# Where and on which queue a spectral mixing kernel loads its filters, and how it shares the products of its first batch

## Chip, cores, metric

One Trainium2 chip, one core of it. The metric is device microseconds of one execution. Three executions of the kernel before gave a median of 1016.6 us (1016.42 to 1018.65). "us" counts from the start of the core's span unless a duration is meant.

## The reference

Eight sequences of 3008 tokens and 256 channels are multiplied by one complex filter in the frequency domain (filters of 1505 frequencies by 256 channels, real and imaginary part in two float32 arrays), then go through an RMS norm and a SwiGLU feed-forward layer.

```python
X = np.fft.rfft(x, axis=1)                       # x: (8, 3008, 256)
y = np.fft.irfft(X * (filt_r + 1j*filt_i), n=3008, axis=1)
rms = np.sqrt(np.mean(y*y, axis=-1, keepdims=True) + 1e-06)
xn = y / rms * rms_g
g = xn @ w_gate                                  # (256, 1536)
out = (g / (1 + np.exp(-g)) * (xn @ w_val)) @ w_out
```

## The kernel before

The transform of 3008 = 47 x 64 points is done in two stages by matmuls. The data change their layout between stages by a "bounce" through a scratch tensor in HBM: they are stored from SBUF (`z_store`) and loaded again in another order (`t2_load`). The parts that matter here:

- `a_unit`: first stage, one matmul and a ScalarE copy. `z_store`, `t2_load`: the first bounce.
- `b_unit(b, i)`: second stage for two of 32 columns, then two products with the filters, `s1 = ps*fr` and `s2 = ps*fi`. `bi_unit`: the first inverse stage of these columns (matmuls `psi`, a ScalarE copy). `g_store`, `t4_load`: the second bounce.
- norm, then for each tile of 512 tokens twelve slots of gate, value and down matmuls. `pg` is a gate matmul. From the first `pg` on, the mixing of the batches 1 to 7 is interleaved with the feed-forward slots of the batch before. Batch 0 has nothing to hide behind; its time up to the first `pg` is the *prologue*.

The filters come in four chunks of eight columns (f0 to f3), each of a real and an imaginary tile of 128 partitions. Rows 0 to 23 and 32 to 54 are loaded, the second group in reversed order; `f_dup` copies the lower half of the partitions to the upper half.

```python
def b_unit(b, i):
    ps = bank(0 if b else i % 2, "psb").rearrange("p (a d) -> p a d", a=2)
    for u in range(2):                       # two matmuls into ps
        ...
    s1 = sp.tile([P, 2, D], FP16, tag="s1", name="s1")
    s2 = sp.tile([P, 2, D], FP16, tag="s2", name="s2")
    c, r = divmod(2 * i, KC)
    nc.vector.tensor_tensor(out=s1, in0=ps, in1=fr[c][:, r:r + 2, :], op=ALU.mult)
    if b == 0 and i % 2:                     # odd units of batch 0: ScalarE copies, GpSimd multiplies
        v = ...
        nc.scalar.activation(out=v, in_=ps, func=AXT.Copy)
        nc.gpsimd.tensor_tensor(out=s2, in0=v, in1=fi[c][:, r:r + 2, :], op=ALU.mult)
    else:
        nc.vector.tensor_tensor(out=s2, in0=ps, in1=fi[c][:, r:r + 2, :], op=ALU.mult)
    st[b]["s"][i] = (s1, s2)

def f_load(c):
    for src, dst in ((filt_r, fr), (filt_i, fi)):
        t = dst[c]
        nc.gpsimd.dma_start(t[0:24, :, :].rearrange("p a d -> p (a d)"),            # 24 rows, 192 KB
                            raw(src, c * KC, [[64 * D, 24], [1, KC * D]]))
        lo = 1 if c == 0 else 0
        for a, e in ((0, 16), (16, 23)):                                            # 16 rows, 7 rows
            nc.gpsimd.dma_start(t[32 + a:32 + e, lo:KC, :],
                                raw(src, 64 * (a + 1) - c * KC - lo,
                                    [[64 * D, e - a], [-D, KC - lo], [1, D]]))
        ...                                                                         # one column more for c == 0

def f_dup(c):
    nc.vector.tensor_copy(out=fr[c][HALF:P], in_=fr[c][0:HALF])
    nc.scalar.activation(out=fi[c][HALF:P], in_=fi[c][0:HALF], func=AXT.Copy)

# the prologue, cut: x on GpSimd's queue, f0 behind it, then
for c in range(NC):
    ...                                      # memsets of fr[c], fi[c]
    for i in range(3):
        a_unit(0, 3 * c + i)
    z_store(0, c)
gate(st[0]["t1"][3][0:1, 5, 0:1])            # GpSimd waits for the last first-stage tile
f_load(1)
...
for c in range(3):
    t2_load(0, c)
gate(st[0]["t2"][0][0:1, 0, 0:1])            # GpSimd waits for the first second load
f_load(2)
...
for i in range(17):
    if i < 16:
        b_unit(0, i)
    if i == 1:
        f_load(3)
    if i == 7:
        w_load(0)                            # half of the weights; the other half at i == 11
    if i == 15:
        for c in range(NXC):
            x_load(1, c)
    if i % 4 == 1 and i // 4 + 1 < NC:
        f_dup(i // 4 + 1)
    if i >= 1:
        bi_unit(0, i - 1)
        if i % 2 == 0:
            g_store(0, i // 2 - 1)
    if i == 4:
        t2_load(0, 3)
```

## Time and profile before

| event (read from the trace) | us |
|---|---|
| f0, f1, f2, f3 landed | 21.1, 27.4, 44.5, 50.3 |
| last z store landed | 28.1 |
| first second load issued, landed | 28.3, 32.2 |
| first product | 35.5 |
| last g store issued, landed | 71.5, 81.1 |
| first gate matmul (end of the prologue) | 94.4 |
| span | 1015.2 |

The windows view gives each engine's busy time in a stretch (with the number of instructions), the granted clock, the mean busy share of the 16 DMA engines, and what they moved. Of the kernel before:

```profile
core 0: us, PE busy (x) PEld busy (x) DVE busy (x) ACT busy (x) POOL busy (x), PEclk, DMA share, GB/s
4.00:20.00 16.00, 7.37 (x27) 2.83 (x27) 13.66 (x12) 8.15 (x16) 9.79 (x20) 1.00 1.04 233
20.00:28.00 8.00, 0.00 (x0) 0.00 (x0) 4.47 (x6) 1.91 (x1) 0.13 (x1) 1.00 0.88 193
28.00:36.00 8.00, 2.90 (x20) 2.12 (x20) 6.04 (x9) 2.06 (x4) 3.44 (x7) 1.00 1.03 193
36.00:44.00 8.00, 4.39 (x19) 2.81 (x20) 5.84 (x9) 4.77 (x6) 5.55 (x9) 1.00 0.91 108
44.00:52.00 8.00, 5.44 (x24) 3.48 (x24) 4.25 (x6) 5.13 (x7) 2.51 (x3) 1.00 0.87 170
...
62.00:74.00 12.00, 5.57 (x25) 3.01 (x22) 2.67 (x4) 3.93 (x7) 8.36 (x14) 1.00 1.17 190
74.00:96.00 22.00, 5.52 (x44) 3.64 (x45) 3.26 (x8) 3.85 (x7) 2.51 (x3) 1.00 0.55 133
96.00:200.00 104.00, 98.60 (x666) 61.40 (x665) 62.94 (x103) 63.97 (x113) 22.73 (x19) 0.98 0.47 109
```

After 96 us TensorE is busy 98.6 of 104 us: little is to be gained there. Before, it has little to do in any row.

The waits view (engine and line, what it waited for: us in total, times, longest), same kernel, 28 to 95 us:

```profile
PE psn L310 <- DMA t_588<-g_tmp: 13.9, 1, 13.9
...
PE psi L232 <- DMA wi<-wi_t: 3.8, 1, 3.8
...
PE psi L232 <- POOL s_364 L222: 2.2, 1, 2.2
...
PE psi L232 <- POOL s_556 L222: 1.9, 1, 1.9
...
PE psi L232 <- POOL s_461 L222: 1.7, 1, 1.7
PE psi L232 <- POOL s_396 L222: 1.7, 1, 1.7
```

TensorE's largest is the inverse bounce (13.9: the last g store alone took 9.66 us to land). The `psi <- POOL` waits of about 2 us come once in each pair of units: an odd unit goes VectorE product, ScalarE copy, GpSimd product, inverse, and only then the next unit's matmul. The GpSimd product itself, by the view of its source line (the three numbers are the shortest, median and longest duration in ns):

```profile
L222 POOL TENSOR_TENSOR s_326<-v,fi_118 x1: 1598/1598/1598, 38.1 to 38.1; 128x512 f16<-128x512 f32 x1
L222 POOL TENSOR_TENSOR s_364<-v,fi_118 x1: 1274/1274/1274, 43.4 to 43.4; 128x512 f16<-128x512 f32 x1
L222 POOL TENSOR_TENSOR s_396<-v,fi_119 x1: 1678/1678/1678, 47.4 to 47.4; 128x512 f16<-128x512 f32 x1
```

### The profile page before, as it was taken

How to read it: one execution, taken by the hardware profiler on the slowest of the kernel's cores; microseconds unless marked ns; L12 is line 12 of the kernel's file. 1: busy time of each engine (PE TensorE's matmuls, PEld its weight loads, DVE VectorE, ACT ScalarE, POOL GpSimd, SP SyncE). 2: the span in 40 equal slices, each digit the busy share in tenths (PEclk: the TensorE clock that was granted, in tenths of full speed). 3: DMA queues.
4: the chain of work that ended last, by engine and by line, in shares of the span. 5: the costliest groups of instructions: out<-in, count | busy, mean ns of one | idle time of the engine just before them, and what ended most of it. 6: DMA issues, size and time to landing. Idle time of an engine off the chain costs nothing.

```text
span 1015.2 us, 17359 instructions
## 1 busy us (share of the span) xinstructions
PE 932.0 (92%) x6279; PEld 570.4 (56%) x6279; DVE 601.0 (59%) x980; ACT 602.4 (59%) x1060; POOL 249.1 (25%) x221
## 2 busy tenths in 40 slices
PE   2444989999999999999999999999999999999997
PEld 1322556655665566655665566655665556656554
DVE  8632467645774477645775467645775467645554
ACT  4443755666655765567555765567656766566543
POOL 5460341032401232032411323031411322023200
PEclk9999999999999999999999999999999999999999
DMA  9994373325723474324824375314724343312211
GB/s 193 165 167 108 87 172 76 102 76 135 151 66 102 96 169 103 99 72 121 164 51 121 86 150 123 107 50 117 162 78 123 86 125 87 101 49 61 43 42 39
DMA packets 94565, 107.25 MB, mean 106 GB/s; under 512 B 17224, under 2 KB 69064, under 8 KB 94288
## 3 DMA queue, kind: packets, MB, share of 16 engines
q1 hardware_dynamic: 85104, 87.59, 33.1%
q0 software_dynamic: 8992, 17.77, 11.7%
q8 instruction: 49, 0.80, 0.3%
q10 hardware_dynamic: 384, 0.79, 0.3%
q14 instruction: 36, 0.29, 0.1%
HBM read 70.88 MB, written 49.90 MB: 119 GB/s over the span
## 4 chain that ended last, share of the span: by engine, by line
PE 75%; DMA 8%; ACT 5%; issue 4%; DVE 3%; POOL 2%; SPq 1%; ACTq 0%; DVEq 0%; POOLq 0%
PE pg L359 21%; PE pv L359 20%; PE psi L232 5%; PE psb L212 3%; PE psn L264 2%; ACT sq L273 1%; SPq L201 1%; PE psa L191 1%; DMA g_tmp<-t_579 1%; DMA xc<-in_x_dram 1%; DVE hh L364 1%; PE psq L281 1%; DMA fi_120<-in_filt_i_dram 1%; ACT y L271 1%; PE po_12769 L376 0%
## 5 line engine op out<-in xcount | busy, mean ns | idle before, releaser
L364 DVE TENSOR_TENSOR hh<-pv,sg 128x512 f16<-128x512 f32 (+1 forms) x576 | 390.9, 679 | 349.5 <-ACT sg L363 224.1
L363 ACT ACTIVATE sg<-pg 128x512 f16<-128x512 f32 (+1 forms) x576 | 340.6, 591 | 308.6 <-PE pg L359 306.2
L359 PE MATMUL pg<-xn,wg 128*128 128x512 f16 (+1 forms) x1152 | 340.1, 377 | 0.0
L359 PE MATMUL pv<-xn,wv 128*128 128x512 f16 (+1 forms) x1152 | 338.9, 376 | 0.0
L376 PEld LDWEIGHTS <-hh 128*128 128x128 f16 (+1 forms) x2304 | 221.6, 98 | 110.6 <-issue 33.2
L339 POOL TENSOR_TENSOR xn<-y,rb 128x1024 f16<-128x1024 f32 (+1 forms) x47 | 129.6, 2758 | 300.8 <-DMA rb<-r_tmp 231.2
L359 PEld LDWEIGHTS <-wv 128*128 128x128 f16 x1152 | 113.1, 98 | 132.0 <-issue 2.2
L293 POOL TENSOR_TENSOR rho<-u,mhalf 128x4 f32<-128x4 f32 x48 | 48.6, 1013 | 376.0 <-DVE u L291 361.0
L359 PEld LDWEIGHTS <-wg 128*128 128x128 f16 x1152 | 105.7, 98 | 21.6
L232 PEld LDWEIGHTS <-wi 128*128 128x128 f16 x512 | 52.1, 103 | 54.2 <-issue 14.7
L271 ACT ACTIVATE y<-psn,gsb 128x512 f32<-128x512 f32 (+1 forms) x94 | 64.3, 684 | 10.4 <-PE psn L264 5.3
L273 ACT ACTIVATE sq<-psn 128x512 f16<-128x512 f32 (+1 forms) x94 | 55.5, 591 | 0.0
L191 PE MATMUL psa<-xc,wa 128*128 128x512 f16 x96 | 37.5, 408 | 10.8 <-DMA xc<-in_x_dram 9.6
L212 PEld LDWEIGHTS <-wb 96*128 96x128 f16 x256 | 24.9, 105 | 36.0 <-issue 15.0
L175 POOL DMA_DIRECT2D xc<-in_x_dram x64 | 34.9, 561 | 0.8 <-POOLq L579 0.8
L281 PEld LDWEIGHTS <-sq 128*128 128x128 f16 (+1 forms) x384 | 17.5, 97 | 14.9 <-ACT sq L312 2.2
L281 PE MATMUL psq<-ones,sq 128*128 128x1 f16 (+1 forms) x384 | 17.7, 165 | 3.7 <-ACT sq L312 1.9
L191 PEld LDWEIGHTS <-wa 128*128 128x128 f16 x96 | 9.3, 100 | 19.3 <-issue 11.7
L425 PE MATMUL pst<-ident,wb 96*128 96x128 f16 x31 | 3.7, 313 | 11.6 <-DMA wb<-wb_t 11.6
L429 DVE TENSOR_SCALAR wi<-pst 64x512 f16<-64x512 f32 (+1 forms) x16 | 10.7, 672 | 5.5 <-ACT wi L427 5.2
L310 PE MATMUL psn<-wai,t_588 128*128 128x128 f16 x8 | 1.0, 308 | 13.9 <-DMA t_588<-g_tmp 13.9
L313 DVE TENSOR_SCALAR y<-psn,gsb 128x512 f32<-128x512 f32 x2 | 1.4, 746 | 19.7 <-ACT sq L312 19.7
(965 smaller groups left out, 1171.3 us busy)
## 6 DMA issues: line engine op xcount, KB each, us to landing
rb<-r_tmp SPq DMA_DIRECT2D x47, 256.0 KB, 4.0
xc<-in_x_dram POOLq DMA_DIRECT2D x56, 192.0 KB, 5.9
xc<-in_x_dram POOLq DMA_DIRECT2D x8, 160.0 KB, 6.6
wb<-wb_t SPq DMA_DIRECT2D x4, 192.0 KB, 5.6
wg<-in_moe_w_gate_dram POOLq DMA_DIRECT2D x2, 384.0 KB, 5.3
wv<-in_moe_w_val_dram POOLq DMA_DIRECT2D x2, 384.0 KB, 7.2
wo<-in_moe_w_out_dram POOLq DMA_DIRECT2D x2, 384.0 KB, 9.4
r_tmp<-rho SPq DMA_DIRECT2D x47, 2.0 KB, 2.1
```

Of the source, the lines that this page charges most:

```text
L191: nc.tensor.matmul(ps, wa, st[b]["x"][c][:, 2 * r:2 * r + 2, :], start=True, stop=True)
L212: nc.tensor.matmul(ps[:, u, :], wb[:, k, :], st[b]["t2"][k // KC][:, k % KC, :], start=True, stop=True)
L232: nc.tensor.matmul(ps[:, u, :], wi[:, 2 * i + u, q, :], s12[q][:, u, :], start=(q == 0), stop=(q == 1))
L271: nc.scalar.activation(out=y[:, dh, 0:w], in_=ps[:, 0:w], func=AXT.Identity, scale=gsb[:, dh:dh + 1])
L273: nc.scalar.activation(out=st[b]["sq"][m][:, dh, 0:w], in_=ps[:, 0:w], func=AXT.Square)
L281: nc.tensor.matmul(ps[0:w, q:q + 1], sq[:, dh, q * P:q * P + w], ones, start=(dh == 0), stop=(dh == 1))
L293: nc.gpsimd.tensor_tensor(out=rho, in0=u, in1=mhalf, op=ALU.pow)
L339: nc.gpsimd.tensor_tensor(out=xv[:, :, 0:nq], in0=yv[:, :, 0:nq], in1=rv[:, 0:nq].unsqueeze(1).to_broadcast([P, 2, nq, P]), op=ALU.mult)
L359: nc.tensor.matmul(ps[:, 0:w], wt[:, dt_, ts(jt, P)], xn[:, dt_, 0:w], start=(dt_ == 0), stop=(dt_ == 1))
L363: nc.scalar.activation(out=sg[:, 0:w], in_=pg[:, 0:w], func=AXT.Silu)
L364: nc.vector.tensor_tensor(out=hh[:, 0:w], in0=pv[:, 0:w], in1=sg[:, 0:w], op=ALU.mult)
L376: nc.tensor.matmul(po[s4 // 2][0:w, s4 % 2, :], hh[:, s4 * P:s4 * P + w], wo[:, jt, :], start=(jt == 0 and s4 % 2 == 0), stop=(jt == JT - ...
```

## The change

The intent is to empty the store window of filter traffic, to have the tables copied early, to let whole products alternate between VectorE and GpSimd, and to take the inverse off their round trip. So the filters leave GpSimd's queue and stand on SyncE's between the stores and the loads of the first bounce; GpSimd takes both products of odd units; the inverse runs three units behind; x of batch 1 and two thirds of the weights wait for the second bounce.

```diff
 b_unit:
-        nc.vector.tensor_tensor(out=s1, in0=ps, in1=fr[c][:, r:r + 2, :], op=ALU.mult)
+        eng = nc.vector
         if b == 0 and i % 2:
+            eng = nc.gpsimd
             ...                      # ScalarE copies ps to v
+            ps = v
+        eng.tensor_tensor(out=s1, in0=ps, in1=f1, op=ALU.mult)
+        eng.tensor_tensor(out=s2, in0=ps, in1=f2, op=ALU.mult)
 f_load: each of its transfers
-            nc.gpsimd.dma_start(
+            nc.sync.dma_start(
 prologue:
+            if c == 1:               # tables: loaded and copied between the z stores
+                wb_load(2); wb_load(3); wi_group(0); wi_group(1)
+        nc.sync.dma_start(wi[:, 0], wi0_d)
+        f_load(0)                    # all on SyncE's queue, in this order
+        t2_load(0, 0)
+        t2_load(0, 1)
+        f_load(1)
+        t2_load(0, 2)
+        f_load(2)
-        for i in range(17):
+        for i in range(19):
-            if i == 1:
+            if i == 5:
+                t2_load(0, 3)
                 f_load(3)
             if i == 9:
                 w_load(0)            # now a third of the weights
-            if i >= 1:
-                bi_unit(0, i - 1)
+            if i >= 3:
+                bi_unit(0, i - 3)
+        gate(st[0]["t4"][0][0:1, 0, 0:1])
+        w_load(1)
+        w_load(2)
         norm_first()
+        for c in range(NXC):
+            x_load(1, c)
```

Cut: three memsets of filter tiles go to ScalarE, the half of batch 0's `t4` loads that stood on ScalarE's queue leaves it except for the first chunk, and slots of the first norms and of batch 1 shift by a few.

More of the change, by code (lines that the diff above doesn't have):

```diff
@@ L213, in b_unit @@
                              start=True, stop=True)
-        s1 = sp.tile([P, 2, D], FP16, tag="s1", name="s1")
-        s2 = sp.tile([P, 2, D], FP16, tag="s2", name="s2")
         c, r = divmod(2 * i, KC)
-        nc.vector.tensor_tensor(out=s1, in0=ps, in1=fr[c][:, r:r + 2, :], op=ALU.mult)
+        f1, f2 = fr[c][:, r:r + 2, :], fi[c][:, r:r + 2, :]
+        if b:
+            s1 = sp.tile([P, 2, D], FP16, tag="s1", name="s1")
+            s2 = sp.tile([P, 2, D], FP16, tag="s2", name="s2")
+        else:
+            s1, s2 = (hp.tile([P, 512], FP16, tag=g, name=g).rearrange("p (a d) -> p a d", a=2)
+                      for g in ("sg", "hh"))
+        eng = nc.vector
         if b == 0 and i % 2:
+            eng = nc.gpsimd
             v = yp.tile([P, 2, 512], FP32, tag="y", name="v")
@@ L221, in b_unit @@
             nc.scalar.activation(out=v, in_=ps, func=AXT.Copy)
-            nc.gpsimd.tensor_tensor(out=s2, in0=v, in1=fi[c][:, r:r + 2, :], op=ALU.mult)
-        else:
-            nc.vector.tensor_tensor(out=s2, in0=ps, in1=fi[c][:, r:r + 2, :], op=ALU.mult)
+            ps = v
+        eng.tensor_tensor(out=s1, in0=ps, in1=f1, op=ALU.mult)
+        eng.tensor_tensor(out=s2, in0=ps, in1=f2, op=ALU.mult)
         st[b]["s"][i] = (s1, s2)
@@ L248, in t4_load @@
                 r0 = ri * SL + h * H + c * XC
-                (nc.scalar if b == 0 and h else nc.sync).dma_start(t[p0:p0 + 32, :, :],
+                (nc.scalar if b == 0 and c == 0 and h else nc.sync).dma_start(t[p0:p0 + 32, :, :],
                                                                    g_d[b, :, r0:r0 + XC, :])
@@ L405, in f_load @@
             t = dst[c]
-            nc.gpsimd.dma_start(t[0:24, :, :].rearrange("p a d -> p (a d)"),
+            nc.sync.dma_start(t[0:24, :, :].rearrange("p a d -> p (a d)"),
                                 raw(src, c * KC, [[64 * D, 24], [1, KC * D]]))
@@ L409, in f_load @@
             for a, e in ((0, 16), (16, 23)):
-                nc.gpsimd.dma_start(t[32 + a:32 + e, lo:KC, :],
+                nc.sync.dma_start(t[32 + a:32 + e, lo:KC, :],
                                     raw(src, 64 * (a + 1) - c * KC - lo,
@@ L413, in f_load @@
             if c == 0:
-                nc.gpsimd.dma_start(t[32:56, 0, :], raw(src, 32, [[64 * D, 24], [1, D]]))
+                nc.sync.dma_start(t[32:56, 0, :], raw(src, 32, [[64 * D, 24], [1, D]]))
     def f_dup(c):
@@ L438, in w_load @@
     def w_load(q):
-        cols = ts(q, DFF // 2)
+        cols = ts(q, DFF // 3)
         for src, dst in ((moe_w_gate, wg), (moe_w_val, wv)):
             nc.gpsimd.dma_start(dst[:, :, cols], src.rearrange("(dt p) j -> p dt j", p=P)[:, :, cols])
-        nc.gpsimd.dma_start(wo[:, ts(q, JT // 2), :],
-                            moe_w_out.rearrange("(jt p) d -> p jt d", p=P)[:, ts(q, JT // 2), :])
+        nc.gpsimd.dma_start(wo[:, ts(q, JT // 3), :],
+                            moe_w_out.rearrange("(jt p) d -> p jt d", p=P)[:, ts(q, JT // 3), :])
     def wb_load(c):
@@ L449 @@
         nc.vector.memset(mhalf, -0.5)
-        nc.vector.memset(fr[0][0:HALF], 0.0)
-        nc.vector.memset(fi[0][0:HALF], 0.0)
         warm = up.tile([P, 4], FP32, tag="rho", name="warm")
@@ L455 @@
             x_load(0, c)
-        f_load(0)
         nc.sync.dma_start(wa, wa_d)
@@ L461 @@
         for c in range(NC):
-            if c:
-                nc.vector.memset(fr[c][0:HALF], 0.0)
-                nc.vector.memset(fi[c][0:HALF], 0.0)
+            for t in (fr[c], fi[c]):
+                if c < 2 or (c == 2 and t is fr[c]):
+                    nc.vector.memset(t[0:HALF], 0.0)
+                else:
+                    nc.scalar.activation(out=t[0:HALF].rearrange("p a d -> p (a d)"),
+                                         in_=mhalf[0:HALF, 0:1].to_broadcast([HALF, KC * D]),
+                                         func=AXT.Copy, scale=0.0)
+        nc.vector.memset(ones, 1.0)
+        for c in range(NC):
             for i in range(3):
@@ L467 @@
             z_store(0, c)
-        nc.vector.memset(ones, 1.0)
-        gate(st[0]["t1"][3][0:1, 5, 0:1])
-        f_load(1)
-        wb_load(2)
-        wb_load(3)
-        for c in range(3):
-            t2_load(0, c)
-        gate(st[0]["t2"][0][0:1, 0, 0:1])
+            if c == 1:
+                wb_load(2)
+                wb_load(3)
+                wi_group(0)
+                wi_group(1)
+        nc.sync.dma_start(wi[:, 0], wi0_d)
+        f_load(0)
+        t2_load(0, 0)
+        t2_load(0, 1)
+        f_load(1)
+        t2_load(0, 2)
         f_load(2)
-        nc.sync.dma_start(wi[:, 0], wi0_d)
         nc.sync.dma_start(wai, wai_d)
@@ L480 @@
             nc.sync.dma_start(gsb, moe_rms_g.rearrange("(a p) -> p a", p=P))
-        for g in range(4):
+        for g in range(2, 8):
             wi_group(g)
         f_dup(0)
-        for g in range(4, 8):
-            wi_group(g)
-        for i in range(17):
+        for i in range(19):
             if i < 16:
                 b_unit(0, i)
-            if i == 1:
+            if i == 5:
+                t2_load(0, 3)
                 f_load(3)
-            if i == 7:
+            if i == 9:
                 w_load(0)
-            if i == 11:
-                w_load(1)
-            if i == 15:
-                for c in range(NXC):
-                    x_load(1, c)
             if i % 4 == 1 and i // 4 + 1 < NC:
                 f_dup(i // 4 + 1)
-            if i >= 1:
-                bi_unit(0, i - 1)
+            if i >= 3:
+                bi_unit(0, i - 3)
                 if i % 2 == 0:
-                    g_store(0, i // 2 - 1)
-            if i == 4:
-                t2_load(0, 3)
+                    g_store(0, i // 2 - 2)
         for c in range(NXC):
             t4_load(0, c)
+        gate(st[0]["t4"][0][0:1, 0, 0:1])
+        w_load(1)
+        w_load(2)
         norm_first()
@@ L510 @@
         n_unit(0, 1, 1)
-        q_unit(0, 1)
-        rho_move(0, 1)
+        for c in range(NXC):
+            x_load(1, c)
         items = [(b, m, jt) for b in range(B) for m in range(6) for jt in range(JT)]
@@ L525, in norm_plan @@
             at(s0 + 10, xn_unit, b, m)
-        at(4, xn_unit, 0, 1)
+        at(1, q_unit, 0, 1)
+        at(2, rho_move, 0, 1)
+        at(7, xn_unit, 0, 1)
         for m in range(2, 6):
-            norm_plan(0, m, (m - 2) * 10)
+            norm_plan(0, m, 2 + (m - 2) * 9)
         for b in range(1, B):
             t = (b - 1) * 72
-            a0, b0, bs = (6, 22, 7) if b == 1 else (0, 16, 8)
+            a0, b0, bs = (8, 24, 6) if b == 1 else (0, 16, 8)
             for i in range(12):
```

## The prediction

> **What bounds the kernel now.** Two regimes. From 94.4 us on (first gate matmul in the timeline) TensorE is busy 97 to 99% of nearly every stretch, and the change hardly touches that work. Before 94.4 us TensorE is 36 us busy of 95 (windows). This prologue has four parts, read from timeline and chain of waits:
> 1. To 35.5 us: x, first bounce, until the first product. DMA share is about 1.0 at 200 to 220 GB/s from 4 to 28 us, because GpSimd issues filters 0 and 1 (1.5 MB) into the z stores. The second load waits until 28.3 for the last store; then VectorE works 5.6 us on table copies (29.8 to 35.4).
> 2. To 70.9: sixteen units at about 4.3 us a pair. Each odd unit is a serial round trip: VectorE product 0.7, ScalarE copy 0.6, GpSimd product 1.27 (1.68 beside an f32 copy), inverse 0.8, next matmul.
> 3. 71.5 to 84.7: the last g store takes 9.7 us to land, since batch 1's x (1.5 MB) and weights fill the DMA; then loads, 3.4.
> 4. 84.7 to 94.4: first norm.
>
> **What the change does, costed.**
> Part 1: filters leave the store window (1.5 MB at about 215 GB/s, 7 us), but filter 0 (0.75 MB, 3.5) now stands before the second loads on SyncE. Tables are copied earlier. VectorE loses three memsets (1.8 each) to an idle ScalarE. I estimate first product at 28.5 to 29.5: 6 to 7 us gained.
> Part 2: inverse three units behind removes the round trip. GpSimd does two products per odd unit, so it paces: 2 x 1.27 plus gaps, about 2.7 a pair (estimate), 0.4 more beside each f32 copy, plus 2.4 for issuing one third of the weights. That is about 25 instead of 35.4. But bytes also bound it: x, tables, z, filters, second loads, g and a third of the weights make 11 MB, some 51 us at 215 GB/s. I expect 2 to 4 us of stalls where filters 1 and 3 arrive just in time and block VectorE and ScalarE in order. Last g store near 58 to 60.
> Part 3: x(1) and two thirds of the weights wait for the first t4 load; the g store should land in about 3 us instead of 9.7.
> Part 4: the first square no longer waits behind DMA issues on ScalarE (1 us) and q_unit no longer stands before the first gate matmul (1.5), but six weight issues of 0.8 us hold GpSimd before rho (+1 to 2). About 9 us.
> First gate matmul: about 75 instead of 94.4. After it: x(1) now issues behind the weights, so rho of tile 1 comes near 5 us after that matmul, its xn just ahead of need at 17 us: 0 to 3 us may be lost. Batch 1's wait for t2 (3.7 us at 130) stays mostly.
>
> All but the last line lies on the critical path. Predicted 997 us, range 990 to 1004.
>
> [...]
>
> **Would show it right:** first gate matmul at 72 to 78; pairs at 2.6 to 3.2; last g store landing in 2.5 to 4. **Wrong:** SyncE holding second loads or g stores behind filter slot waits; f_dup waiting on DMA over 4 us; GpSimd products slower than 1.3; a TensorE gap over 3 us at tile 1 or batch 1.
>
> Chances: faster by over 2% 0.42, within 2% 0.56, slower 0.02.

The four parts come to a first gate matmul at about 75 instead of 94.4, and to 997 us.

## More of the kernel before

The DMA columns tell two different stories. At 4 to 20 us the engines are full and move 233 GB/s, x, filters and z stores together. At 36 to 44 us, where nearly only filters move, they are just as full (0.91) and move 108.

## The result and the profile after

The changed kernel took 1012.86 us, median of four (1011.66 to 1013.84); the kernel before, on the same chip, 1017.24 (1016.42 to 1018.65). The ratio is 0.9955, interval 0.9936 to 0.9974: within 2%, outside the predicted range of 990 to 1004. A ratio is the mean time of one kernel's runs over that of the other's of the same rounds, so not quite the ratio of the medians. Executions over 1.5% slower than the fastest of the same kernel are left out of the means.

| event | before | predicted | after |
|---|---|---|---|
| last z store landed | 28.1 | | 20.2 |
| first second load landed | 32.2 | | 31.6 |
| first product | 35.5 | 28.5 to 29.5 | 32.3 |
| f0, f1, f2, f3 landed | 21.1, 27.4, 44.5, 50.3 | | 29.2, 43.1, 51.9, 61.4 |
| last g store issued | 71.5 | 58 to 60 | 73.9 |
| it took to land | 9.66 | about 3 | 2.26 |
| first gate matmul | 94.4 | 75 | 86.4 |
| span | 1015.2 | | 1009.9 |

The windows view of the changed kernel:

```profile
core 0: us, PE busy (x) PEld busy (x) DVE busy (x) ACT busy (x) POOL busy (x), PEclk, DMA share, GB/s
4.00:20.00 16.00, 7.52 (x43) 3.44 (x44) 12.57 (x15) 13.35 (x23) 1.79 (x5) 0.95 0.95 238
20.00:28.00 8.00, 0.00 (x0) 0.00 (x0) 5.85 (x8) 0.38 (x1) 0.00 (x0) 0.50 0.98 133
28.00:36.00 8.00, 2.87 (x13) 1.68 (x13) 1.29 (x2) 2.50 (x2) 2.48 (x2) 0.50 1.16 125
36.00:44.00 8.00, 1.78 (x8) 1.03 (x8) 3.11 (x4) 0.76 (x1) 0.00 (x0) 0.50 0.91 113
44.00:52.00 8.00, 2.88 (x12) 1.69 (x12) 3.23 (x4) 3.20 (x5) 5.91 (x4) 0.50 0.77 132
...
62.00:74.00 12.00, 7.78 (x40) 5.03 (x39) 3.60 (x6) 8.71 (x14) 8.81 (x8) 0.72 0.77 135
74.00:96.00 22.00, 13.04 (x96) 7.99 (x97) 6.84 (x14) 8.82 (x16) 11.15 (x18) 0.69 1.00 192
96.00:200.00 104.00, 95.23 (x646) 59.42 (x644) 63.13 (x104) 61.71 (x108) 23.86 (x20) 0.98 0.52 117
```

From 20 to 52 us the DMA share is as high as before, but the rate fell to 113 to 133 GB/s where it had been 193, 193, 108 and 170. The granted clock column reads 0.50 where before it read 1.00, but the clock records of the trace before begin only at 99 us. Matmuls of one form run at the same pace in both traces there (0.42 us for a 128x256 one), and TensorE has 7.5 us of work in these 32, so the clock explains nothing. The waits view, 28 to 95 us:

```profile
PE psb L212 <- DMA t_241<-z_tmp: 11.9, 1, 11.9
...
ACT fi_119 L424 <- DMA fi_119<-in_filt_i_dram: 9.9, 1, 9.9
...
ACT fi_118 L424 <- DMA fi_118<-in_filt_i_dram: 8.9, 1, 8.9
PE psi L238 <- ACT t_350 L243: 8.5, 1, 8.5
...
PE psn L316 <- DMA t_568<-g_tmp: 6.4, 1, 6.4
...
DVE fr_115 L423 <- DMA fr_115<-in_filt_r_dram: 5.7, 1, 5.7
PE psi L238 <- ACT t_390 L243: 5.0, 1, 5.0
...
ACT fi_120 L424 <- DMA fi_120<-in_filt_i_dram: 4.8, 1, 4.8
PE psi L238 <- ACT t_455 L243: 4.5, 1, 4.5
...
ACT fi_121 L424 <- DMA fi_121<-in_filt_i_dram: 3.5, 1, 3.5
DVE fr_116 L423 <- DMA fr_116<-in_filt_r_dram: 3.5, 1, 3.5
```

The bounce at the end shrank from 13.9 to 6.4 us. In exchange there is a new family: `fi_119`, `fi_120`, `fi_121` and their `fr` partners are the `f_dup` copies of chunks 1, 2 and 3, waiting for their load. In the trace ScalarE takes the inverse's own copies (`t_350`, `t_390`, `t_455`) only after the `f_dup` copy that stands before them in its program, and TensorE waits 8.5, 5.0 and 4.5 us for them: 18 us. The store window gave up 7.9 us (last z store at 20.2 instead of 28.1) and the first product came only 3.2 us earlier.

Where its filter had landed, the changed loop ran as intended. The first of the two GpSimd products in the source-line view, again the shortest, median and longest in ns:

```profile
L229 POOL TENSOR_TENSOR sg<-v,fr_114 x2: 1258/1262/1265, 33.5 to 45.8; 128x512 f16<-128x512 f32 x2
...
L229 POOL TENSOR_TENSOR sg<-v,fr_117 x2: 1265/1266/1267, 67.7 to 70.2; 128x512 f16<-128x512 f32 x2
```

The second product took 1.25 to 1.27 us too, but for one (timeline view: start, duration), which began beside VectorE's `f_dup` copy of `fr_116` (49.39 to 50.64 us):

```profile
49.52 2.24 POOL L230 TENSOR_TENSOR hh<-v,fi_119 128x512 f16<-128x512 f32 x1
```

From 64 to 73 us a pair of units takes 2.5 us, where it had been about 4.3.

After the prologue, TensorE's waits from 94 to 180 us, before and then after:

```profile
PE psb L212 <- DMA t_1085<-z_tmp: 3.7, 1, 3.7
PE psq L281 <- ACT sq L273: 0.9, 1, 0.9
```

```profile
PE psb L212 <- DMA t_1135<-z_tmp: 4.6, 1, 4.6
PE pg L365 <- POOL xn L345: 2.0, 1, 2.0
PE po_1248 L382 <- DVE o_1234 L389: 0.8, 1, 0.8
PE psb L212 <- ACT sq L279: 0.7, 1, 0.7
```

The prologue gained 8.0 us and the span 5.3. The 2.7 between went into these waits: by the gate matmul of slot 12 the lead had shrunk from 8.0 to 7.0, by slot 36 to 5.3.

### The profile page after: what moved, and what is told of

It reads as the page before. It is cut to its first block, busy times and chain, and to the rows that moved or that the text cites. A ratio compares the mean times of both kernels' runs of the same rounds, so it can differ in the third digit from the quotient of the medians.

```text
span 1009.9 us, 17370 instructions
## 1 busy us (share of the span) xinstructions
PE 927.2 (92%) x6279; PEld 568.1 (56%) x6279; DVE 592.3 (59%) x969; ACT 607.6 (60%) x1063; POOL 246.7 (24%) x205
## 4 chain that ended last, share of the span: by engine, by line
PE 73%; DMA 7%; ACT 4%; issue 3%; DVE 3%; POOL 1%; SPq 1%; ACTq 0%; DVEq 0%; POOLq 0%
PE pg L365 21%; PE pv L365 20%; PE psi L238 5%; PE psb L212 3%; PE psn L270 1%; ACT sq L279 1%; SPq L201 1%; PE psa L191 1%; DMA wv<-in_moe_w_val_dram 1%; ACT y L277 1%; PE psq L287 1%; DMA r_tmp<-rho 1%; DVE hh L370 1%; ACT sg L369 1%; PE po_12770 L382 0%
## 5 line engine op out<-in xcount | busy, mean ns | idle before, releaser
L238 PE MATMUL psi<-sg,wi 128*128 128x256 f16 x32 | 12.1, 381 | 18.2 <-ACT t_350 L243 8.5
L238 PE MATMUL psi<-hh,wi 128*128 128x256 f16 x32 | 12.0, 380 | 1.5 <-POOL hh L230 1.5
```

The costliest lines, as they stand in the source:

```text
L238: nc.tensor.matmul(ps[:, u, :], wi[:, 2 * i + u, q, :], s12[q][:, u, :], start=(q == 0), stop=(q == 1))
```

## The experiments

Eighteen kernels were run. The theories changed on the way, and the texts use their letters: K packet size, S an uneven spread of a transfer over the DMA engines (my reading of its completion updates; no trace shows the engine of a packet), D and P (in e5 to e10, and again in e17 and e18) the partitions that a transfer goes to, O the filters' order and rate, Q one queue with eight transfers outstanding (in the changed kernel's trace f2's first transfer went out at 35.91 us, when `t_243`, issued eight transfers before it, had landed at 35.85); other letters are explained in their texts. Kernels "wrong on purpose" compute with other filter rows; they ran once, so their state is unknown, and they are judged by the times of the prologue in their profile. As a common measure I take from each trace the stretch from the landing of the first second load to the landing of f2: two second loads and two chunks of filters pass in it on one queue. e15 and e16 were executed a second time, and the traces kept are of that execution (spans 998.9 and 999.9 us; the timed ones had 996.1 and 1001.9); their events are read from the kept traces.

### Undoing one part of the change: e4, e8, e14 (e7)

**e4_products_only**: the kernel before, with only the alternating products and the inverse three units behind.

```diff
-            nc.gpsimd.tensor_tensor(out=s2, in0=v, in1=fi..., op=ALU.mult)   # s1 on VectorE
+            both products on GpSimd in odd units (as in the change)
-            if i >= 1: bi_unit(0, i - 1)
+            if i >= 3: bi_unit(0, i - 3)
```

> The kernel before with only the products changed (even units on VectorE, odd units on GpSimd, inverse three units behind, their tiles from the other pool); filters, weights, x and all loads as before. Before: first product 35.5 us, last g store issued 71.5, first gate matmul 94.4. Theory that the product change is good by itself and was masked by late filters: pairs at 2.7 to 3.0 us where filters have landed, last g store issued at 63 to 66, first gate matmul at 86 to 89, time 1008 to 1012. Rival P (the products pace the loop and gain nothing): last g store at 70 or later, time 1015 to 1018.

Measured: 1013.66 us, ratio 0.9972 (0.9947 to 0.9997); last filter 50.8, last g store issued at 66.2 and 9.6 us in landing, first gate matmul 89.3. The products alone bring the prologue 5.1 us, at the old filter times.

**e8_filters_as_before**: the changed kernel, but the filters on GpSimd's queue at the places of before.

```diff
 f_load:
-            nc.sync.dma_start(
+            nc.gpsimd.dma_start(
 prologue:
+        f_load(0)                                   # behind x, before the z stores
-        f_load(0); t2_load(0, 0); t2_load(0, 1); f_load(1); t2_load(0, 2); f_load(2)
+        gate(st[0]["t1"][3][0:1, 5, 0:1]); f_load(1)
+        t2_load(0, 0); t2_load(0, 1); t2_load(0, 2)
+        gate(st[0]["t2"][0][0:1, 0, 0:1]); f_load(2)
```

> The changed kernel with all filter loads back where the kernel before had them (GpSimd queue, filters 0 and 1 during the first bounce's stores, 2 after the first second-load, 3 after the first product); the products, weights, x and the rest as changed (right result). If the move of the filters out of the store window is what ate the gain (theories D and S agree: a slow transfer that ran beside others now runs alone on the critical path): filter 3 lands at 50 to 53 instead of 61.4, last g store issued at 63 to 67 instead of 73.9, first gate matmul at 76 to 80, time 1001 to 1007 us. If the filters' place does not matter: first gate matmul at 84 to 88.

Measured: 1002.78 us (1002.24 to 1004.18), ratio 0.9865 (0.9844 to 0.9887). First product 32.9, last filter 50.9, last g store issued at 64.5 and 2.27 us in landing, first gate matmul 77.2. Its windows:

```profile
core 0: us, PE busy (x) PEld busy (x) DVE busy (x) ACT busy (x) POOL busy (x), PEclk, DMA share, GB/s
...
20.00:28.00 8.00, 2.07 (x16) 1.65 (x17) 5.30 (x8) 4.08 (x5) 0.00 (x0) 0.50 0.82 201
28.00:36.00 8.00, 3.19 (x14) 1.99 (x14) 4.35 (x6) 2.60 (x3) 3.35 (x6) 0.50 0.96 185
36.00:44.00 8.00, 2.88 (x12) 1.68 (x12) 4.55 (x7) 2.82 (x5) 7.88 (x11) 0.50 0.87 127
```

201 GB/s at 20 to 28 us, where the changed kernel has 133. So the move of the filters costs 9.2 us of prologue (86.4 against 77.2) and 10 us of time inside the change. Without it the change is as fast as any correct kernel: e9, e17 and e18 (ratios 0.9864 to 0.9869) cannot be told from it.

**e7_filters_only**, the opposite: the kernel before with the filters' move alone.

> The kernel before with one part of the change: the filters leave GpSimd's queue and stand on SyncE's, at the places of the changed kernel (f0 ahead of the second loads, f1 before the third, f3 behind the fourth). Theory O (filters issued after the stores move at 100 to 140 GB/s and set the pace): last filter landed 60 to 63 us instead of 50.3, and since the products still go in serial round trips, the last g store is issued at 73 to 76 (71.5 before), first gate matmul at 95 to 99 (94.4), time 1018 to 1022 us against 1017. Rival R (the move by itself gains, because the second loads start early, and the loss in the changed kernel comes from its meeting with the faster products): first product 32 to 33, last g store at 67 to 69, first gate matmul at 90 to 92, time 1012 to 1015 us.

Measured: 1030.62 us, first gate matmul 106.5. It was spoilt: the table `wi[:, 0]` that the first inverse needs had stayed behind the filters on SyncE's queue and landed at 50.8, and TensorE waited 16.8 us for it. The right edit puts it ahead, as the change does:

```diff
+        nc.sync.dma_start(wi[:, 0], wi0_d)
         f_load(0); t2_load(0, 0); t2_load(0, 1); f_load(1); t2_load(0, 2); f_load(2)
-        nc.sync.dma_start(wi[:, 0], wi0_d)
```

> e7 mended: in e7 the table that the first inverse needs had been left behind the filters on SyncE's queue, which held the first inverse until 50.9 us and with it the fourth second load and filter 3. Here it stands before filter 0, as in the changed kernel; so this is the kernel before with the filters' move alone. Theory O (the filters' order and rate set the pace): filter 3 landed 60 to 64 us, last g store issued at 73 to 77, first gate matmul 95 to 99 (94.4 before), time 1018 to 1022 us. Rival R (the move alone gains): first product 32 to 33, last g store at 67 to 69, first gate matmul 90 to 92, time 1012 to 1015 us.

**e14_filters_only_wi** measured 1023.35 us, ratio 1.0067 (1.0047 to 1.0088); f3 landed at 61.3, last g store issued at 76.1, first gate matmul 98.0. The move alone loses: its first second load, issued 3.7 us earlier, landed at 31.6 us instead of 32.2, which does not pay for the late filters.

### What is slow about the filters: queue, packets, rows (e3, e1, e13)

**e3_filters_gpsimd**: the changed kernel, the same order, but the filters on GpSimd's queue (`nc.gpsimd.dma_start`, with gates in their places).

> The changed kernel with only the filter loads put back on the GpSimd queue, held back by a 1-element copy of a SyncE-loaded table so that they still come after the first bounce's stores (right result). If the queue's kind or its order is what ate the gain (theories K, S and Q alike): filter 1's last piece lands at 33 to 36 instead of 43.1, filter 3 at 46 to 52 instead of 61.4, the sixteen units then take 26 to 30 us, first gate matmul at 76 to 80, time 1000 to 1006 us. If rather the alternating products or the inverse three units behind are slow (rival P: GpSimd's two products or ScalarE's in-order copies pace the loop), the first gate matmul stays at 84 to 88 and the time at 1010 to 1014.

Measured: 1014.16 us, ratio 0.9969 (0.9941 to 0.9998), first gate matmul 86.4. The second load landed at 24.6 because no filter stood before it, but f0 landed at 36.2 and f3, issued late behind GpSimd's products, at 61.3. So the order is not quite the same, but a filter's tiles still landed 3.0 to 3.5 us apart (f0 and f1). The kind of queue is not the cause.

**e1_rows_forward** (wrong): the reversed rows read forward, so that their packets are 8 KB rather than 1 KB.

```diff
-                                        [[64 * D, e - a], [-D, KC - lo], [1, D]]))
+                                        [[64 * D, e - a], [1, (KC - lo) * D]]))
```

> The changed kernel, but the reversed filter rows are read forward, as contiguous runs of 8 KB instead of eight runs of 1 KB (wrong result on purpose; same bytes, same rows per DMA, same queue and order). In the changed kernel filter 1's last piece lands at 43.1 us, filter 3's at 61.4, and the first gate matmul starts at 86.4. Theory K (small packets: 1 KB packets at about 120 ns each are the cost): filter 1 lands by about 34, filter 3 by about 48, first gate matmul at 74 to 78. Theory S (uneven spread: [...]13 and 8 completion updates instead of 16): [...]filter 1 still lands after 39 and the first gate matmul stays at 83 or later. Theory Q (everything in one queue with eight DMAs outstanding, whatever their form): no change, within 1.5 us of 86.4.

Measured: f1 43.4, f3 61.5, first gate matmul 86.6 (86.4). Packet size is not the cause.

**e13_rows_close** (wrong): the same transfers from neighbouring rows, 8 KB apart rather than 64.

```diff
-                                raw(src, c * KC, [[64 * D, 24], [1, KC * D]]))
+                                raw(src, c * 24 * KC, [[KC * D, 24], [1, KC * D]]))
                                 # and the reversed groups likewise
```

> Wrong on purpose. The changed kernel with the same filter transfers (same count, same bytes, same destinations, same queue and places), but each reads neighbouring rows of the filter, 8 KB from one partition to the next, where the changed kernel reads rows that lie 64 KB apart. Theory M (the reads at a stride of 64 KB are what holds the filters to 100 to 140 GB/s when they are alone): filter 1 landed by 32 to 35 us (43.1), filter 3 by 46 to 50 (61.4), last g store issued at 58 to 62 (73.9), first gate matmul 71 to 75 (86.4), time 996 to 1000 us. Rival[...]: filter 1 at 41 to 44, filter 3 at 59 to 62, first gate matmul 84 to 87, time 1010 to 1013 us.

Measured: f3 65.7, first gate matmul 90.7, 1014.89 us. No gain (rather worse); the distance of the rows is not the cause.

### What is slow about the filters: rows per transfer and partitions (e2, e6, e5, e9, e10)

**e2_sixteen_rows** and **e6_sixteen_narrow** (both wrong): three transfers of 16 rows to partitions 0, 32 and 48 instead of 24, 16 and 7; and only two of them, to 0 and 32.

```diff
-            t[0:24]  <- 24 rows ;  t[32:48] <- 16 rows ;  t[48:55] <- 7 rows
+            t[0:16]  <- 16 rows ;  t[32:48] <- 16 rows ;  t[48:64] <- 16 rows     # e2: 384 KB
+            t[0:16]  <- 16 rows ;  t[32:48] <- 16 rows                            # e6: 256 KB
```

> The changed kernel, but each filter DMA has 16 rows (16 forward, 16 and 16 reversed; wrong result on purpose): 384 KB instead of 376 KB a filter chunk, with more 1 KB packets (256 instead of 184), on the same queue in the same order[...]. Theory S (uneven spread): [...]all filter DMAs show 16 completion updates; filter 1 lands by about 37 instead of 43.1, filter 3 by about 52 instead of 61.4, first gate matmul at 77 to 81 instead of 86.4. Theory K (small packets): 39% more of them, so filter 1 lands at 43 to 48 and the first gate matmul at 86 to 92. Theory Q (one queue, eight outstanding): within 1.5 us of 86.4.

> The changed kernel with two filter DMAs of 16 rows a filter and chunk (forward into partitions 0 to 15, reversed into 32 to 47; wrong result on purpose): [...]256 KB instead of 376 KB[...]. Theory S (DMA engines): at least as fast as the even run with three DMAs of 16 rows: filter 1's last piece by 34, filter 3's by 48, first gate matmul at 75 to 78. Theory D[...]: about as slow as the changed kernel, filter 1's last piece at 39 to 44, filter 3's at 56 to 62, first gate matmul at 83 to 87.

Measured: e2 had its f3 at 53.5 and the first gate matmul at 78.5; e6 at 48.6 and 74.1. I first took this for S, since in the changed kernel's trace a transfer of 24 rows gives 13 completion updates, one of 16 rows 16 and one of 7 rows 8 (on GpSimd's queue, in the kernel before, each gives 16). That fewer updates mean fewer DMA engines was my assumption, which no trace shows. And as an explanation of the rate S was a misreading, as the next runs showed. e6 was fast because it moved a third less: its 256 KB took 1.9 to 2.4 us a filter, mean 2.2 or 119 GB/s (e2: 384 KB in 3.0 us, 131 GB/s).

**e5_imag_upper**, **e9_before_upper** (both correct) and **e10_even_both_halves** (wrong): the imaginary filter loaded to partitions 64 to 127 and copied down; in the changed kernel, in e8, and in e2 with real and imaginary pieces in turn.

```diff
-            t = dst[c]
+            t = dst[c] if dst is fr else dst[c][HALF:P]
-    nc.scalar.activation(out=fi[c][HALF:P], in_=fi[c][0:HALF], func=AXT.Copy)
+    nc.scalar.activation(out=fi[c][0:HALF], in_=fi[c][HALF:P], func=AXT.Copy)
```

> The changed kernel, but the imaginary filter is loaded into partitions 64 to 119 and copied down, instead of into 0 to 55 and copied up (right result). Same DMAs, same rows, same queue, order and completion counts; only the destination partitions of half the filter bytes differ. The real filter still goes to 0 to 55. Theory D ([...]alone they moved at about 115 GB/s in the run with filters on GpSimd): [...]filter 1's last piece lands at 34 to 38 instead of 43.1, filter 3's at 48 to 54 instead of 61.4, first gate matmul at 76 to 81 instead of 86.4, time 1002 to 1007 us. Theory S (uneven spread over DMA engines, 13, 16 and 8 completion updates): unchanged, first gate matmul at 85.5 to 87.5, time 1010 to 1014.

> The run with all filter loads back as before, and the imaginary filter into the upper 64 partitions (right result): a version that might beat both kernels. Theory D: the filters cost less DMA time in the store window too, so the stores land earlier and filters 2 and 3 too; first gate matmul at 73 to 77, 2 to 4 us ahead of the run without the upper half, time 998 to 1004 us. Theory S: no difference from that run, within 1 us.

> The run with three even DMAs of 16 rows a filter and chunk on SyncE, plus the imaginary filter into partitions 64 to 127, real and imaginary pieces issued in turn so that both halves are filled at the same time (wrong result on purpose, same bytes as the even run). While only filters moved, every run so far showed 100 to 140 GB/s. Theory D[...]: [...]filters alone move at 180 GB/s or more; filter 1's last piece lands by 34 instead of 37.2, filter 3's by 48 instead of 53.5, first gate matmul at 73 to 76 instead of 78.5. Rival H (the limit is not on the destination side): rate alone stays at 110 to 140, landings within 1 us, first gate matmul at 77.5 to 79.

Measured: e5 1008.07 us, ratio 0.992 (0.9894 to 0.9945), first gate matmul 82.2, short of what D asked (see its text); e9 1003.14, no different from e8; e10 first gate matmul 77.9 against 78.5 in e2. From e10 I concluded that the destination is not the limit. That conclusion was wrong too: two transfers in turn to two halves test whether transfers add up, not whether one transfer is limited by the partitions that it goes to.

### One transfer over more partitions: e15, e16

Each chunk of each filter (384 KB) in one transfer, over 64 partitions (e15, the form in which x is loaded) or over 48 (e16). Both wrong; all else is the changed kernel.

```diff
-            three transfers of 24, 16 and 7 rows
+            nc.sync.dma_start(dst[c][0:64, 0:6, :], raw(src, 6 * c, [[22 * D, 64], [D, 6], [1, D]]))   # e15
+            nc.sync.dma_start(dst[c][0:48, 0:8, :], raw(src, 8 * c, [[30 * D, 48], [D, 8], [1, D]]))   # e16
```

> Wrong on purpose. The changed kernel with each filter's chunk read by one transfer over 64 partitions, six rows of 1 KB each (384 KB; 376 in the changed kernel), which is the form of the x loads: x moved at about 200 GB/s by itself. Theory N (the division into three transfers of 24, 16 and 7 partitions is what holds the filters' rate down): filters alone at 180 GB/s or more, filter 1 landed by 32 to 35 us (43.1 in the changed kernel, 37.2 in e2), filter 3 by 46 to 50 (61.4, 53.5 in e2), first gate matmul 71 to 75 (86.4, 78.5 in e2). Rival (the rate has nothing to do with the form, and the even spread of e2 is all there was to gain): filter 1 at 36 to 38, filter 3 at 52 to 55, first gate matmul 77 to 79.

> Wrong on purpose. As e15, but one transfer over 48 partitions with eight rows each (384 KB), so the same partitions and row counts as e2, which had three transfers of 16 partitions. Theory N1 (the number of transfers counts): as fast as e15, filter 3 by 46 to 50 us and first gate matmul at 71 to 75. Theory N2 (the partitions that one transfer is spread over count, 64 as against 48): slower than e15, near e2, filter 3 at 51 to 54, first gate matmul at 76 to 79.

Windows of e15's timed execution (the kept trace of the second one has 195, 216 and 210 GB/s in these rows):

```profile
core 0: us, PE busy (x) PEld busy (x) DVE busy (x) ACT busy (x) POOL busy (x), PEclk, DMA share, GB/s
...
20.00:28.00 8.00, 0.35 (x3) 0.26 (x2) 6.03 (x9) 2.64 (x3) 0.00 (x0) 0.50 1.01 200
28.00:36.00 8.00, 4.36 (x20) 2.51 (x18) 5.58 (x7) 3.34 (x4) 2.64 (x3) 0.50 1.10 223
36.00:44.00 8.00, 5.63 (x26) 3.58 (x26) 3.96 (x5) 5.71 (x9) 7.45 (x6) 0.50 0.98 209
```

200 to 223 GB/s where the changed kernel has 113 to 133. In the kept trace the filters of chunks 1 and 2 land 1.8 to 2.0 us after the load before them: 384 KB at about 212 GB/s. f3 landed at 45.95, last g store issued at 59.6, first gate matmul 72.7; the one timed run took 997.85 us. With 48 partitions it is 2.0 to 2.6 us, mean 2.4 (161 GB/s), first gate matmul 76.5. The cause lies in the form of the transfer. Its division into three is a smaller part of it: e16 is e2 in one piece and beats it by 1.9 us.

### Partitions or their spread: e17, e18

By the mean distance of the landings of f1's and f2's tiles from the load before them, a filter took 3.2 us in the changed kernel (24, 16 and 7 neighbouring rows), 3.0 in e2, 2.2 in e6, 2.4 in e16 and 1.85 in e15.

e15 and e16 changed the number of partitions together with their spread. e17 separates the two and is a correct kernel: the rows stand on every fourth partition, in transfers of 16, 8, 8 and 15 rows. None has more than 16 partitions (24 before), but they spread over 61, 29, 29 and 57; the rows and columns of the tables are permuted to match.

```diff
 _make_tables: place of row s among partitions 0 to 63
-                sign, q = 1.0, s
+                sign, q = 1.0, 4 * s if s < 16 else 4 * s - 63
-                sign, q = -1.0, 32 + s - 24
+                sign, q = -1.0, 4 * s - 63 if s < 32 else 4 * s - 126
 f_load:
+            t = dst[c][0:HALF].rearrange("(g r) a d -> g r a d", r=4)
+            for g, n, r, row in ((0, 16, 0, 0), (0, 8, 1, 16)):         # forward rows
+                nc.sync.dma_start(t[g:g + n, r, :, :].rearrange("g a d -> g (a d)"),
+                                  raw(src, 64 * row + c * KC, [[64 * D, n], [1, KC * D]]))
+            for g, n, r, row in ((8, 8, 1, 1), (0, 15, 2, 9)):          # reversed rows
+                ...
```

> Correct. The changed kernel with the filters' rows laid out otherwise over partitions 0 to 63, every fourth partition, by transfers of 16, 8, 8 and 15 rows[...]; the tables' rows and columns are permuted to match.[...] Theory P ([...] e16's 48 partitions gave 2.5, e15's 64 gave 1.9): 1.8 to 2.2 us a filter, filter 1 landed by 34 to 37 us (43.1), filter 3 by 48 to 52 (61.4), last g store issued at 60 to 64 (73.9), first gate matmul 73 to 77 (86.4), time 997 to 1001 us. Rival N (the number of partitions in one transfer counts, which falls here from 24 to 16 at most): 3.4 us a filter or more, filter 3 at 60 to 64, first gate matmul at 85 to 90, time 1011 to 1015 us.

Measured: 1004.33 us (1003.24 to 1005.95), ratio 0.9864 (0.9844 to 0.9884). The filters of chunk 1 landed 1.64 us apart (second load 35.10, then 36.74 and 38.38), those of chunk 2 1.9 and 2.0 (40.84, 42.78, 44.78). That is not yet a rate, since pieces of a filter had moved before the load ahead of it landed. By the packets that began in the stretch (32.53 to 44.78 us) e17 moved 165 GB/s with its DMA engines busy 0.73; e2, with 16 neighbouring rows in each transfer, needs a share of 1.16 for 147. e18 below against e8 shows the same on GpSimd's queue: while f2 moved, 128 GB/s at a share of 0.49 (33.01 to 36.85 us) against 126 at 0.85 (36.40 to 43.13). So rows spread over the partitions cost the DMA engines little more than half the time, with no more partitions in a transfer than e2 has. Why the spread helps, no run shows. Windows of e17:

```profile
core 0: us, PE busy (x) PEld busy (x) DVE busy (x) ACT busy (x) POOL busy (x), PEclk, DMA share, GB/s
...
20.00:28.00 8.00, 0.00 (x0) 0.00 (x0) 6.03 (x8) 0.68 (x2) 0.00 (x0) 0.50 0.32 93
28.00:36.00 8.00, 3.42 (x15) 1.96 (x15) 1.29 (x2) 2.50 (x2) 1.64 (x2) 0.50 0.85 176
36.00:44.00 8.00, 3.29 (x15) 1.93 (x14) 4.94 (x6) 3.96 (x5) 3.75 (x4) 0.50 0.68 169
```

The row of 20 to 28 us shows why the whole fell short of its expectation by one to three us (f3 53.1, last g store 65.6, first gate matmul 78.0): the DMA engines are busy 0.32 of it. SyncE issues the twelve transfers of f0 at about 0.7 us each, so issuing is what takes the time there, and the first second load goes out at 28.2 instead of 23.4.

e18 is e8 with the same rows (`nc.gpsimd.dma_start`).

> Correct. e8 (everything changed except the filters' queue and times, so far the fastest correct kernel, 1002.8 us) with the rows of e17. Theory P: the store window shortens[...] (last z store landed at 25 to 27 us, 28 in before), filter 3 by 46 to 48 us (50.9 in e8), first gate matmul 73 to 76 (77.2), time 998 to 1001 us. Rival N: as e8 or slower, since GpSimd issues eight transfers a chunk instead of six: first gate matmul 77 to 80, time 1002 to 1005 us.

Measured: 1004.68 us, ratio 0.9869 (0.9847 to 0.9891); no faster than e8. Its last z store landed at 24.5 (28.4 in e8), its first product came at 29.5 (32.9), f3 at 48.4, about as P expects. But the first gate matmul came at 76.8 (77.2): GpSimd spends 29.4 to about 34.5 us on issuing f2, and its first products wait behind that. The gain was lost again, most likely to that wait on the engine that issues.

### Two more on the order of transfers: e12, e11

**e12_filters_earlier**: e8 with f1, f2 and f3 each one gate earlier.

```diff
             z_store(0, c)
+            if c == 0:
+                gate(st[0]["t1"][0][0:1, 5, 0:1]); f_load(1)      # f2 at the next gate, f3 at the one after
```

> e8 (everything changed except the filters' queue and times) with filters 1, 2 and 3 issued one stage earlier: filter 1 when the first first-stage tile is ready, filter 2 when the last is, filter 3 when the first second load has landed. Theory O (filters are fast only while other queues' stores and loads move beside them, so putting more of them in the store window hides more): filter 2 landed by 36 to 40 us (44 to 46 before), filter 3 by 44 to 47 (50.9 in e8), last z store landed 29 to 31 (28 before), last g store issued at 60 to 63 (64.5 in e8), first gate matmul 73 to 76 (77.2), time 998 to 1001 us. Rival B (total bytes set the first 50 us; what the filters gain the stores and second loads lose): first product 36 to 38 instead of 33 to 35, last g store at 64 to 66, first gate matmul 77 to 79, time 1002 to 1005 us, as e8.

Measured: 1007.56 us, ratio 0.9896 (0.9881 to 0.9911). f3 landed at 48.3, but the last z store at 34.4 and the first product came at 39.2: worse than either theory expected. More filters in the store window delayed the stores (28.4 in e8), and with them all that follows; e8's placement is better.

**e11_x_later**: e8 with x of batch 1 issued at slot 3, after the norm statistics of tile 1, and the mixing of batch 1 moved accordingly. It is aimed at the waits after the prologue.

```diff
-        for c in range(NXC):
-            x_load(1, c)                     # before the first gate matmul
+            at(3, x_load, 1, c)
-            a0, b0, bs = (8, 24, 6) if b == 1 else (0, 16, 8)
+            a0, b0, bs = (12, 30, 5) if b == 1 else (0, 16, 8)
```

> The run with all filters as before (1002.8 us), with batch 1's x loaded behind the second tile's norm instead of ahead of it, batch 1's stages 4 to 6 slots later and tighter, and batch 2's x 16 slots later (right result). After the first gate matmul that run lost 2.4 us to the kernel before: TensorE waited 2.4 for tile 1's xn (its rho stood behind x issues that wait for weights; its 2 KB store then took 5.8 to land) and 4.3 for batch 1's second load against 3.7. If these waits are the loss: tile 1's wait under 0.5, batch 1's wait under 2, first gate matmul unchanged at 76.5 to 78, time 997 to 1000.5 us. If a_unit then waits for x instead: a TensorE gap of 1 to 3 us at slot 12, time 1000 to 1003.

Measured: 1004.8 us (1000.2 to 1007.52), ratio 0.9873 (0.9845 to 0.9901): no gain on e8. The wait for tile 1's `xn` stayed at 2.4 us, that of batch 1's second load went from 4.3 to 3.1. The run does not decide whether x delays tile 1: rho's little store was issued at 84.21, x at 84.14, and the broadcast load behind it landed at 95.9 (94.9 in e8), so that it met x either way.

### The stretch in one table

| kernel | transfers of one filter | stretch, us | GB/s | DMA share | 8 KB packet, ns |
|---|---|---|---|---|---|
| after | 24, 16, 7 rows | 20.3 | 118 | 0.87 | 833 |
| e1 (8 KB packets) | same | 20.6 | 118 | 0.86 | 856 |
| e13 (rows close) | same | 23.1 | 110 | 0.89 | 918 |
| e5 (imaginary to 64..127) | same | 18.2 | 130 | 0.91 | 863 |
| e2 | 16, 16, 16 | 16.4 | 147 | 1.16 | 768 |
| e10 (e2, halves in turn) | 16, 16, 16 | 15.8 | 156 | 1.16 | 745 |
| e6 | 16, 16 | 13.1 | 146 | 1.17 | 934 |
| e16 | 48 | 14.1 | 174 | 1.10 | 775 |
| e17 | 16, 8, 8, 15 | 12.3 | 165 | 0.73 | 580 |
| e15 | 64 | 11.3 | 205 | 1.06 | (6 KB) 466 |

Rates and shares are those of the windows view for the stretch, so they count the packets that began in it; the last column is the mean of the packet records there. Where a transfer's rows are spread (e17, e15), a packet itself is quick (580 and 466 ns). One thing stays open. By their landings the changed kernel's filters took 3.2 us each and e2's 3.0, but the two second loads among the changed kernel's took 4.2 and 3.3 us, where e15's took 2.1 and 1.8; and e2, whose rows are no more spread, is 3.9 us faster over the stretch. Its DMA engines are busy 1.16, those of the changed kernel 0.87. An uneven division over the engines (S) as a second and smaller cause would fit this, but no trace shows such a division and no run separates it.

## Why the prediction was wrong

**The step that failed** is the rate of the filters: "filter 0 (0.75 MB, 3.5) now stands before the second loads", and again in "bytes also bound it: ... some 51 us at 215 GB/s. I expect 2 to 4 us of stalls". 215 GB/s was read at 4 to 28 us, a mixture of x (64 partitions a transfer), stores and filters. Filters by themselves had shown 108 at 36 to 44 us in the profile before. f0 landed 9.0 us after the last z store instead of 3.5, the first product 3 us late for the prediction. The filters arrived at 43.1, 51.9 and 61.4, and the stalls that they caused, through ScalarE's order, were 18 us instead of 2 to 4. That the term, and not the mechanism, was wrong is shown by e15: the changed program, only with filter transfers that do move at 200 GB/s, has its first product at 28.6 (predicted 28.5 to 29.5), last g store at 59.6 (58 to 60), first gate matmul at 72.7 (75), and took 997.85 us (997) in its one timed run, when the kernel before took 1020.15. TensorE's waits for the inverse's copies fell from 18 us to 5.9 there. No run moved the `f_dup` copies to a later place, so what their place by itself costs is open.

**The reason behind it**, as far as the runs show, is that neighbouring rows on few partitions move slowly (e2's 147 GB/s at a share of 1.16 against e17's 165 at 0.73; e8's 126 at 0.85 against e18's 128 at 0.49). The prediction took the move to another queue to change the order of the transfers and not their rate, without a trace to show it. In e3 this held: nearly the same order on the other queue gave the same 86.4, with a filter's tiles 3.0 to 3.5 us apart there too. But order was exactly what cost: in the kernel before, the slow transfers ran beside z stores and x, and 233 GB/s moved in all; in line on one queue, each held up what stood behind it. e8 against the changed kernel prices this at 9.2 us of prologue.

**Right:** with their filter present, pairs take 2.5 us (predicted 2.7; the sign, 2.6 to 3.2, was just missed), and GpSimd's product 1.26 us. Beside a float32 copy it was slower: 1.68 in the profile before, and once 2.24 in the changed kernel, where 0.4 more had been allowed for it. The last g store landed in 2.26 us (about 3). e4 and e8 show both: 5.1 us from the products alone, 17.2 from all but the filters' move, near the 19.4 predicted for the whole, though not in the predicted place: e8's first product came 2.6 us early, not 6 to 7.

**Right as a range:** "0 to 3 us may be lost" after the prologue; 2.7 were, in tile 1's `xn` (2.0) and batch 1's second load (4.6 instead of 3.7). **Luck:** from the last g store's issue to the first gate matmul the changed kernel took 12.5 us, where 15 to 17 were predicted; this hid a part of the miss, which had been 14 to 16 us at that store (73.9 against 58 to 60).

**The signs named in the prediction** told the failure well: `f_dup` waiting on DMA for over 4 us, first gate matmul outside 72 to 78. The other fears came true in part: one GpSimd product took 2.24 us, and g stores beside f3 took up to 7.8 us to land (issued at 55.0, landed at 62.8). What these cost is not shown.

The prediction was off by 16 us: 11.4 in the prologue (86.4 against 75), and the 2.7 after it that its central figure had not deducted; the remaining 2 are not attributed.

## What to carry to other kernels

Cost a transfer with the rate at which transfers of its own form moved by themselves in the trace, not with the rate of a stretch in which others ran beside it; the DMA share was about 0.9 both at 108 and at 193 GB/s. Before moving loads out of a crowded window, ask whether they are slow ones that the window hid: put in line on one queue, they delay what is behind them. If rows must be loaded in small groups, spreading them over the partitions by stride raised the rate here from 118 to 165 GB/s at a lower DMA share (0.73 instead of 0.87), but each further transfer costs its issue (about 0.7 us in e17). In the end e17, with spread rows, and e8, which left the filters in the stores' shadow, are equally fast (ratios 0.9864 and 0.9865).
